# A fused attention and gated-MLP kernel: two of four float32-score pairs become split pairs, the others are filled to 128 rows, ACT copies out all float32 attention, and half of w_in is converted later

## The chip, the core and the metric

The program runs on one core of a Trainium2 chip. The core has a matrix engine (TensorE, here PE, with its weight loads shown as PEld) and four others that work beside it: VectorE (DVE), ScalarE (ACT), GpSimd (POOL) and SyncE (SP), which here only issues transfers. Each engine runs its own instructions in order and waits on semaphores for the others. The metric is the device time of one execution, in microseconds; smaller is better.

## The reference

Eight batches of eight heads, 576 tokens, 64 features a head. Attention is causal with a decay of the key's distance, and its output is the input `x` of a gated MLP (d_model 512, d_ff 1024).

```python
scores = scale * q @ k.T + (cum[i] - cum[j])      # cum = cumsum(log(clip(f, 1e-4, 1)))
attn   = softmax(causal(scores));  x = attn @ v   # (8, 576, 512) after joining heads
h = relu(x @ w_in);  u, v = h[..., :512], h[..., 512:]
v_n = (v - mean(v)) / sqrt(var(v) + 1e-6)
v_s = w_spatial @ v_n (over tokens) + b_spatial
out = (u * v_s) @ w_out
```

All arrays come as float32, but w_in and w_out arrive in HBM as 64-bit words, and the kernel itself turns each 64-bit number into float32 parts.

## The kernel before

**Pairs.** Two heads form a pair; there are 32 pairs `P`, four to a batch. For each pair and head `h` the kernel computes the scores of four query blocks of 128 rows (widths 128, 256, 384, 512; the causal part only) and one joint "tail" for the last 64 rows of both heads (two tiles of 288 columns). DVE takes each score tile out of PSUM with mask and running minimum (line 264, tile `tt`, numbered tt_94 for the first head and tt_95 for the second in the tables below; the tail is `tl`), ACT does the exponential (266), POOL divides by the row sum (274), PE transposes the result (`tp`, 320 and 333), and ACT or DVE copies it to SBUF (`ef`, or `eh` and `el`). `attend` multiplies with v into PSUM (`x`), and ACT and DVE split the result into a rounded part and a rest, `xh` and `xl` (368, 369).

**Three kinds of number.** PE multiplies plain float32, or a rounded form (fp32r) that needs fewer passes. A value is therefore often split into a rounded part and a rest, and a product is then a sum of fp32r products. Early pairs are not split:

- pairs with `P < NQ` (0 to 3) take their scores in float32: one table `ta` (called `tf`) per head with 64 rows of q and k and 2 rows of decay, 66 rows in all, loaded directly by two SP transfers;
- the other pairs are split: `split` loads `raw`, ACT rounds it to `hi` (210), POOL makes `lo` (212), and six SP transfers per head build the tables `ta` (128 rows) and `tb` (68 rows); the scores are the sum of two fp32r products;
- pairs with `P < NF` (0 to 4) use float32 attention: the transposed scores are copied once, to `ef`, and multiplied once. `evac` alternates these copies between ACT and DVE.

**The tables' slots.** `ta` and `tb` have two buffers each, one per head. A head's table for pair P+1 can be loaded only when pair P's scores and tail are done.

**The MLP.** `moe(b)` needs the four pairs of batch b. It computes v (20 groups of products in 512 columns, `ps`), normalizes it on DVE, ACT and POOL, computes u (in 256 and 320 columns), multiplies v by w_spatial (`sph`, `spl`), gates, and multiplies by w_out.

**The weights.** `load64` turns a piece of a 64-bit matrix into a rounded part and a rest: one load on SP, an absolute value on ACT (141), five steps on DVE (142 to 148), a sum on POOL (149), a rounding on ACT (150), and a subtraction on POOL (151). The v half of w_in is converted by `load_first` in four pieces of 512 columns, together with w_spatial. The u half (eight chunks of 256 elements a partition, `load_rest`) and w_out (eight more) follow. A load of such a chunk carries a `mark`: an earlier instruction after which the scheduler is told to place it. It sets the order of the program and is no semaphore.

**What sets the order.** The loops at the end record attention and MLP interleaved by estimated costs; then the framework's scheduler, with a timeline of its own, orders each engine's instructions. So an edit in one place moves instructions elsewhere. During pairs 0 to 3 there is no MLP work to run beside attention.

Of the kernel before, what the change touches and what calls it, by code (L numbers as in the profile page):

```python
# [8 lines left out]
F32 = mybir.dt.float32  # L9
# [8 lines left out]

BIG = 1.0e9
NF = 5  # L20
NQ = 4
LEAD = 0.25
S = 576
D = 64
# [5 lines left out]
QK = 640 + S  # L30
# [3 lines left out]
def f32(ap):  # L34
    return ap.bitcast(F32)
# [3 lines left out]
def attn_gmlp_kernel(ctx: ExitStack, tc: tile.TileContext, qk, v, f, w_in, w_sp, b_sp, w_out, out):  # L39
# [8 lines left out]
    PPB = NPAIR // B  # L48
# [3 lines left out]
    wk = ctx.enter_context(tc.tile_pool(name="wk", bufs=1))  # L52
# [4 lines left out]
    V, A, G, T, SY = nc.vector, nc.scalar, nc.gpsimd, nc.tensor, nc.sync  # L57
# [123 lines left out]
    def load_rest(n, w_v, dh, dl, tag, bufs):  # L181

        raw = mo.tile([128, NJ, 64, 2], U32, name="w64", tag=("gt0", "gt1", "o")[n % 3], bufs=1)
        w = mo.tile([128, NJ, 64], U32, name="w32", tag=tag, bufs=bufs)
        t = mo.tile([128, NJ, 64], U32, name="wa", tag=tag, bufs=bufs)
        c = slice(64 * n, 64 * n + 64)
        load64(w_v[:, :, c, :], dh[:, :, c], dl[:, :, c], raw, w[:], t[:])


    tt = [cst.tile([128, 1280], F32, name=f"tt{h}") for h in range(2)]  # L190
# [2 lines left out]
    ET = {"f": cst.tile([128, 2, 1600], F32, name="ef", tag="eh")}  # L193
# [3 lines left out]
    def mm(o, l, r, st, sp):  # L197
        T.matmul(o, l, r, start=st, stop=sp)  # L198
# [3 lines left out]
    def split(P):  # L202

        if P < NQ:
            return
# [9 lines left out]
    def prep(P, h):  # L215

        p = slice(64 * h, 64 * h + 64)
        if P < NQ:
            ta = wk.tile([66, QK], F32, name="tf", tag="ta", bufs=2)
            SY.dma_start(out=ta[0:64, :], in_=qk[P, p, :])  # L220
            last['dma', P, h] = SY.dma_start(out=ta[64:66, :], in_=r0s[0][32 * h + P:32 * h + P + 1])
            tab[P, h] = (ta,)
            return
        hi, lo = parts[P]
        ta = wk.tile([128, QK], F32R, name="ta", tag="ta", bufs=2)
        tb = wk.tile([128, QK], F32R, name="tb", tag="tb", bufs=2)
        SY.dma_start(out=f32(ta[0:64, :]), in_=hi[p, :])
        SY.dma_start(out=f32(ta[64:128, 0:640]), in_=lo[p, 0:640])
        SY.dma_start(out=f32(ta[64:128, 640:QK]), in_=hi[p, 640:QK])
        SY.dma_start(out=f32(tb[0:64, 0:640]), in_=hi[p, 0:640])  # L230
        SY.dma_start(out=f32(tb[0:64, 640:QK]), in_=lo[p, 640:QK])
        SY.dma_start(out=f32(tb[64:68, :]), in_=rows_v[:, P, h, :])
        tab[P, h] = (ta, tb)
# [12 lines left out]
    def qkt(o, P, h, q0, k0, n, first, final):  # L246

        k0 += 640
        ts = tab[P, h]
        for t in ts:  # L250
            r = 66 if len(ts) == 1 else 128 if t is ts[0] else 68
            mm(o, t[0:r, q0:q0 + 128], t[0:r, k0:k0 + n], first and t is ts[0], final and t is ts[-1])

    def scores(P, h):
# [43 lines left out]
                            op0=ALU.mult, op1=ALU.mult)  # L298
        yield 0

    nev = [0]

    def evac(P, ps, sel):
        if P < NF:
            (V.tensor_copy if nev[0] % 2 == 1 else A.copy)(sel(ET["f"]), ps)  # L305
            nev[0] += 1
            return
        h_ap, l_ap = sel(ET["h"]), sel(ET["l"])
        A.copy(h_ap, ps)  # L309
        V.tensor_tensor(out=l_ap, in0=ps, in1=f32(h_ap), op=ALU.subtract)  # L310
# [65 lines left out]
    def attention(b, ws=None):  # L376
        for P in range(b * PPB, (b + 1) * PPB):
# [15 lines left out]
            if nxt:  # L393
                prep(P + 1, 0)
                prep(P + 1, 1)
# [28 lines left out]
    def moe(b):  # L424
# [55 lines left out]
        if b == 0:  # L480
            for n in range(8):
                load_rest(n, wo_v, woh, wol, 'GH', 3)
# [77 lines left out]
    for n in range(8):  # L560
        load_rest(n, win_v, winh, winl, 'U', 9)
# [52 lines left out]
```

## Time and profile before

| | |
|---|---|
| timed runs | 813.99, 815.69, 815.85 us, median 815.69 |
| profiled execution | 813.26 us, of which the span of the core's instructions is 811.5 |
| mean granted PE clock | 0.985 |
| busy in the span | PE 788.3 (97%), PEld 704.9, DVE 567.1 (70%), ACT 535.2 (66%), POOL 478.1 (59%) |
| DMA | 103.50 MB, mean 128 GB/s |
| pair 0's attention copied out by ACT | second head 48.23 to 48.65 us |
| pair 3's | 97.43 to 97.85 us |
| pair 5's | 156.13 to 156.55 us |

The share of busy time is an average over very different stretches. What the change touches lies in the first 160 us, where the pairs 0 to 5 and the first MLP run, so the stretches between the times of the last three rows tell more than the whole. Busy time of PE counts matmuls with modelled ends, and at half the granted clock a matmul takes twice as long.

### The profile page before, as it was taken

The numbers are of one execution on the slowest core, as the hardware profiler recorded it, in microseconds if no ns is written. First come the engines' busy times: TensorE is split into PE (matmuls) and PEld (weight loads), VectorE is DVE, ScalarE is ACT, GpSimd is POOL, SyncE is SP. The second block draws the span as 40 slices with busy tenths as digits, with TensorE's granted clock in tenths as the row PEclk, the third lists the DMA queues.
The fourth block names the chain that finished last, engine by engine and source line by source line (L and its number), as shares of the span: only waits on it lengthen the run. The fifth ranks groups of instructions, "written<-read, shape, count | busy, mean of one in ns | idle before, by whom it ended". The sixth has DMA issues, their size and how long they took to land.

```text
span 811.5 us, 15566 instructions
## 1 busy us (share of the span) xinstructions
PE 788.3 (97%) x4980; PEld 704.9 (87%) x4980; DVE 567.1 (70%) x1726; ACT 535.2 (66%) x1432; POOL 478.1 (59%) x677
## 2 busy tenths in 40 slices
PE   7999899999999999999999999999999999999997
PEld 3676678998899989998799989999899988999996
DVE  5879989676976668766776668776786658765321
ACT  5587668676776667666686667776687657764431
POOL 4767788655766647555775537566675547643151
PEclk8699999999999999999999999999999999999999
DMA  7547754456545554565554565556554664430001
GB/s 201 143 121 208 197 140 116 120 151 165 139 122 135 135 146 117 128 166 140 125 141 112 150 152 126 123 144 151 131 130 107 163 164 111 95 77 14 27 1 66
DMA packets 47476, 103.50 MB, mean 128 GB/s; under 512 B 6961, under 2 KB 15153, under 8 KB 47330
## 3 DMA queue, kind: packets, MB, share of 16 engines
q1 hardware_dynamic: 47074, 101.98, 49.8%
q8 instruction: 40, 0.66, 0.3%
q10 hardware_dynamic: 320, 0.52, 0.3%
q14 instruction: 42, 0.34, 0.1%
HBM read 39.41 MB, written 10.68 MB: 62 GB/s over the span
## 4 chain that ended last, share of the span: by engine, by line
PE 87%; DVE 5%; POOL 2%; ACT 2%; DMA 2%; issue 1%; SPq 0%; ACTq 0%; POOLq 0%; DVEq 0%
PE ps L198 47%; PE sc L198 16%; PE x L198 12%; PE tp L320 8%; PE tp L198 2%; PE tp L333 2%; DMA out_dram<-o 1%; POOL tt L274 1%; DVE w L145 1%; ACT tt L266 1%; DVE tt L264 1%; DVE eh L342 0%; DVE wa L142 0%; DVE ef L305 0%; DMA w<-in_dram 0%
## 5 line engine op out<-in xcount | busy, mean ns | idle before, releaser
L274 POOL TENSOR_SCALAR tt<-tt,sm 128x128 f32<-128x128 f32 (+3 forms) x256 | 138.3, 558 | 94.7 <-DVE sm L270 86.4
L264 DVE CUSTOM_DVE_ANT_0 tt<-sc,zm 128x128 f32<-128x128 f32 (+3 forms) x256 | 122.4, 485 | 82.4 <-PE tp L320 63.0
L309 ACT CAST eh<-tp 128x512 fp32r<-128x512 f32 (+1 forms) x270 | 111.5, 425 | 87.2 <-PE tp L320 52.5
L266 ACT ACTIVATE tt<-tt,nm 128x128 f32<-128x128 f32 (+3 forms) x256 | 144.4, 565 | 26.5 <-DVE nm L264 21.5
L310 DVE TENSOR_TENSOR el<-tp,eh 128x512 fp32r<-128x512 f32 (+1 forms) x270 | 127.9, 485 | 25.0 <-ACT eh L309 22.8
L320 PE MATMUL tp<-ident,tt 128*128 128x128 f32 x640 | 113.7, 280 | 1.3 <-DVE ef L305 0.6
L198 PE MATMUL sc<-ta 128*128 128x128 f32 (+1 forms) x336 | 107.8, 327 | 3.9 <-DVE nm L264 3.8
L198 PE MATMUL x<-eh,vt 128*128 128x320 f32 (+4 forms) x378 | 104.5, 287 | 2.7 <-POOL vt L243 1.8
L198 PE MATMUL sc<-tb 68*128 68x128 f32 (+1 forms) x336 | 104.6, 316 | 0.0
L212 POOL TENSOR_TENSOR lo<-raw,hi 128x640 fp32r<-128x640 f32 (+1 forms) x56 | 83.2, 1506 | 18.5 <-ACT hi L210 18.4
L505 POOL TENSOR_TENSOR gl<-u,gh 128x256 fp32r<-128x256 f32 x64 | 47.2, 738 | 79.3 <-ACT gh L504 76.1
L198 PE MATMUL x<-el,vt 128*128 128x256 f32 x324 | 93.4, 306 | 0.0
L320 PEld LDWEIGHTS tp<-ident,tt 128*128 128x128 f32 x640 | 76.8, 142 | 10.9 <-ACT ef L305 1.2
L198 PEld LDWEIGHTS x<-eh,vt 128*128 128x128 f32 x378 | 71.2, 189 | 5.8 <-POOL vt L243 2.7
L198 PE MATMUL ps<-sph,vnh 128*128 128x256 f32 (+1 forms) x240 | 73.3, 306 | 0.2 <-ACT o L530 0.2
L198 PE MATMUL ps<-sph,vnl 128*128 128x256 f32 (+1 forms) x240 | 71.4, 298 | 0.0
L198 PEld LDWEIGHTS sc<-ta 128*128 128x128 f32 x336 | 63.5, 189 | 9.1 <-DVE nm L264 4.9
L198 PE MATMUL ps<-spl,vnh 128*128 128x256 f32 (+1 forms) x240 | 71.2, 296 | 0.0
L198 PE MATMUL ps<-xh,winh 128*128 128x256 f32 (+1 forms) x232 | 70.1, 302 | 0.1
L198 PE MATMUL ps<-xl,winh 128*128 128x256 f32 (+1 forms) x232 | 68.9, 297 | 0.0
L368 ACT CAST xh<-x 64x256 fp32r<-64x256 f32 (+1 forms) x128 | 49.8, 392 | 28.4 <-PE x L198 26.9
L198 PE MATMUL ps<-xh,winl 128*128 128x256 f32 (+1 forms) x232 | 68.4, 295 | 0.0
(190 smaller groups left out, 2127.8 us busy)
## 6 DMA issues: line engine op xcount, KB each, us to landing
raw<-in_dram SPq DMA_DIRECT2D x28, 608.0 KB
ta<-hi SPq DMA_DIRECT2D x56, 304.0 KB
vraw<-in_dram SPq DMA_DIRECT2D x32, 320.0 KB
tb<-hi SPq DMA_DIRECT2D x56, 160.0 KB
ta<-lo SPq DMA_DIRECT2D x56, 160.0 KB
out_dram<-o SPq DMA_DIRECT2D x32, 256.0 KB
ta<-hi SPq DMA_DIRECT2D x56, 144.0 KB
tb<-lo SPq DMA_DIRECT2D x56, 144.0 KB
```

The costliest lines, as they stand in the source:

```text
L145: V.scalar_tensor_tensor(out=w, in0=hi, scalar=0xC0000000, in1=a, op0=ALU.bitwise_and, op1=ALU.bitwise_or)
L198: T.matmul(o, l, r, start=st, stop=sp)
L212: G.tensor_tensor(out=lo[:, c], in0=raw[:, c], in1=f32(hi[:, c]), op=ALU.subtract)
L264: V.tensor_tensor_reduce(out=t, in0=sc[:, 0:n], in1=zm[:, 640 - n:640], scale=-0.125, scalar=3.0e38, op0=ALU.add, op1=ALU.min, accum_out=n ...
L266: last["exp", P, h, i] = A.activation(t, t, AF.Exp, bias=nm[:, i:i + 1], scale=-1.0, accum_out=sm[:, i:i + 1])
L274: G.tensor_scalar(out=t, in0=t, scalar1=sm[:, i:i + 1], scalar2=1.0, op0=ALU.mult, op1=ALU.mult)
L309: A.copy(h_ap, ps)
L310: V.tensor_tensor(out=l_ap, in0=ps, in1=f32(h_ap), op=ALU.subtract)
L320: T.transpose(out=tp[:, (i - c) * 128:(i - c + 1) * 128], in_=tt[h][:, TOFF[i] + 128 * c:TOFF[i] + 128 * c + 128], identity=ident)
L333: T.transpose(out=tp[:, j * 128:(j + 1) * 128], in_=tl[:, c * 128:(c + 1) * 128], identity=ident)
L368: last[P, h] = A.copy(hi, ps[m0:m0 + 64, 0:n])
L505: G.tensor_tensor(out=gl[j][:, 0:256], in0=g[:, 0:256], in1=f32(gh[j][:, 0:256]), op=ALU.subtract)
```

## The change

There are four edits.

1. `NQ` goes from 4 to 2: pairs 2 and 3 are now split pairs like the later ones.
2. The float32 tables of pairs 0 and 1 get 128 rows: DVE clears rows 64 to 127 (the memset is recorded ahead of the transfers, and the two decay rows then overwrite rows 64 and 65), and the products run over 128 rows instead of 66.
3. All copies of float32 attention out of PSUM are done by ACT.
4. The loads of `load_rest` get a mark: chunk n of the u half of w_in (and of w_out) comes after the exponential of pair 3, head n // 4, block n % 4.

```diff
-NQ = 4
+NQ = 2
+NPAD = 2
...
-        load64(w_v[:, :, c, :], dh[:, :, c], dl[:, :, c], raw, w[:], t[:])
+        load64(w_v[:, :, c, :], dh[:, :, c], dl[:, :, c], raw, w[:], t[:], ("exp", PPB - 1, n // 4, n % 4))
...
-            ta = wk.tile([66, QK], F32, name="tf", tag="ta", bufs=2)
+            ta = wk.tile([128, QK], F32, name="tf", tag="ta", bufs=2)
+            if P < NPAD:
+                V.memset(ta[64:128, :], 0.0)
...
-            r = 66 if len(ts) == 1 else 128 if t is ts[0] else 68
+            r = (128 if P < NPAD else 66) if len(ts) == 1 else 128 if t is ts[0] else 68
...
     def evac(P, ps, sel):
         if P < NF:
-            (V.tensor_copy if nev[0] % 2 == 1 else A.copy)(sel(ET["f"]), ps)
-            nev[0] += 1
+            A.copy(sel(ET["f"]), ps)
             return
```

The lines of the new program are shifted by one to three (264 becomes 267, 142 becomes 143). What the scheduler makes of it is seen in the order of the instructions. On DVE, at the start of the program, before (`wa` and `w` are tiles of the weights' conversion, `ISA tt_94` is the first score tile's eviction, `r_114` and `rt` are the decay rows):

```order
L100 TENSOR_SCALAR ft<-ft 64x576
L85 MEMSET r_114 32x2x64 x2
L103 SCALAR_TENSOR_TENSOR r_114<-ones,ft 64x576
L89 COPY r_114<-r_114 64x512
L85 MEMSET rt 32x4x64 x2
L142 TENSOR_SCALAR wa<-wa 128x512
L144 TENSOR_SCALAR wa<-wa 128x512
L264 ISA tt_94,nm<-sc,zm 128x128
```

The same place after:

```order
L222 MEMSET tf 64x1216 x2
L101 TENSOR_SCALAR ft<-ft 64x576
L86 MEMSET r_114 32x2x64 x2
L86 MEMSET rt 32x4x64 x2
L104 SCALAR_TENSOR_TENSOR r_114<-ones,ft 64x576
L90 COPY r_114<-r_114 64x512
L267 ISA tt_94,nm<-sc,zm 128x128
```

The clearing of two tables is new, the clearing of `rt` moved ahead of the scan, and the conversion steps moved behind the first score tiles. On PE, at the end of pair 0's second head, where pair 2's scores begin, before (`x` is attention's output in PSUM):

```order
L198 MATMUL x_403<-ef,vraw 128x256
L198 MATMUL sc<-tf 128x128
L198 MATMUL x_403<-ef,vraw 128x128
L320 MATMUL tp<-ident,tt_94 128x128 x7
```

and after:

```order
L199 MATMUL x_414<-ef,vraw 128x256
L199 MATMUL sc<-ta 128x128
L199 MATMUL sc<-tb 128x128
L199 MATMUL x_414<-ef,vraw 128x128
L320 MATMUL tp<-ident,tt_94 128x128
```

One float32 score product became two split ones, with the transposes of pair 1 cut into smaller groups behind. On DVE, the first conversion of a chunk of w_in's u half, before, between the score tiles of pair 2's second head:

```order
L264 ISA tt_95,nm<-sc,zm 128x384
L264 ISA nm 128x1
L305 COPY ef<-tp 128x128
L142 TENSOR_SCALAR wa<-wa 128x256
L144 TENSOR_SCALAR wa<-wa 128x256
L145 SCALAR_TENSOR_TENSOR w_946<-w_945,wa 128x256
L264 ISA tt_95,nm<-sc,zm 128x512
```

and after, between those of pair 4's second head:

```order
L273 RECIPROCAL sm<-sm 128x4
L143 TENSOR_SCALAR wa<-wa 128x256
L145 TENSOR_SCALAR wa<-wa 128x256
L146 SCALAR_TENSOR_TENSOR w_1008<-w_1007,wa 128x256
L294 TENSOR_SCALAR sm<-sm 128x1
L148 TENSOR_SCALAR wa<-w_1008 128x256
L295 RECIPROCAL sm<-sm 128x1
L149 SCALAR_TENSOR_TENSOR wa<-w_1007,wa 128x256
L267 ISA tt_95,nm<-sc,zm 128x384
```

The conversions moved behind by two pairs, and the copy `ef` is gone from DVE.

More of the change, by code (lines that the diff above doesn't have):

```diff
@@ L299, in scores_tail @@
         yield 0
-    nev = [0]
     def evac(P, ps, sel):
         if P < NF:
-            (V.tensor_copy if nev[0] % 2 == 1 else A.copy)(sel(ET["f"]), ps)
-            nev[0] += 1
+            A.copy(sel(ET["f"]), ps)
             return
```

## The prediction

> **What bounds the kernel now.** I read the stretches first. They are cut where ACT has copied out the attention of pair 0 (48.6 us), pair 3 (97.8, from where moe(0) can run) and pair 5 (156.5); I call them A to E. Columns: stretch, its length, busy us of PE, PEld, DVE, ACT, POOL (instructions), granted PE clock, DMA share, GB/s.
>
> ```profile
> 0.00:13.70 13.70, 9.18 (x32) 3.79 (x32) 5.11 (x13) 6.93 (x12) 8.03 (x19) 0.95 0.84 245
> 13.70:48.60 34.90, 34.24 (x110) 23.03 (x111) 27.67 (x83) 21.08 (x58) 22.79 (x26) 0.68 0.46 122
> 48.60:97.80 49.20, 44.51 (x220) 31.73 (x219) 44.84 (x147) 36.02 (x104) 37.22 (x48) 1.00 0.70 188
> 97.80:156.50 58.70, 55.63 (x364) 50.03 (x363) 51.18 (x140) 38.25 (x103) 44.50 (x63) 1.00 0.56 138
> 156.50:811.50 655.00, 644.74 (x4260) 596.37 (x4258) 438.28 (x1346) 432.88 (x1159) 365.57 (x524) 1.00 0.48 120
> ```
>
> E is 98% PE with DVE at 67%: there only PE's work counts, and by PE's order the two programs run alike from pair 11 on. So the change is decided in A to D. In B PE is 98% busy, but at a clock of 0.68. In C PE and DVE stand at 90% and 91% together. D is PE at 95% with DVE at 87%. Second view, the clock inside B (same columns), and third the chain of what ended last:
>
> ```profile
> 11.00:13.70 2.70, 0.15 (x1) 0.00 (x0) 1.08 (x5) 0.88 (x2) 0.00 (x0) 0.76 1.39 418
> 13.70:33.70 20.00, 19.96 (x43) 12.53 (x44) 15.73 (x48) 10.77 (x31) 12.74 (x14) 0.50 0.47 120
> 33.70:36.20 2.50, 2.50 (x11) 2.17 (x9) 2.43 (x3) 0.62 (x1) 1.41 (x1) 0.50 0.77 168
> 36.20:40.00 3.80, 3.18 (x17) 2.06 (x17) 3.23 (x13) 1.96 (x5) 2.58 (x3) 0.99 0.67 211
> PE 87%; DVE 5%; POOL 2%; ACT 2%; DMA 2%; issue 1%; SPq 0%; ACTq 0%; POOLq 0%; DVEq 0%
> ```
>
> For 22.5 us PE is full and gets half its clock. The work there is mostly float32 scores with 66 rows; the clock returns right after 2.5 us of transposes and `x` products with 128 rows. Such work at full clock would take 11.3 us less.
>
> **The start (A).** Rows: start, duration, engine.
>
> ```profile
> 3.51 0.81 DVE L100 TENSOR_SCALAR ft<-ft 64x576 f32<-64x576 f32 x1 [2.07 <-DMA ft<-in_dram]
> 3.96 1.47 POOL L82 MEMSET rt<- 64x1280 f32 x1
> 5.07 1.35 DVE L103 TENSOR_TENSOR_SCAN r<-ones,ft 64x576 f32<-64x576 f32 x1 [0.39 <-ACT ft L101]
> 12.59 0.43 DVE L142 TENSOR_SCALAR wa<-wa 128x512 f32<-128x512 f32 x1 [5.01 <-ACT wa L141]
> 13.39 0.28 DVE L264 CUSTOM_DVE_ANT_0 tt<-sc,zm 128x128 f32<-128x128 f32 x1
> 13.74 2.07 PE L198 MATMUL sc<-tf 66*128 66x512 f32 x2 [2.59 <-DVE nm L264]
> L97 DVE MEMSET ones<- 64x576 f32 x1 | 0.5, 538 | 0.9 <-PEq L600 0.9
> L85 DVE MEMSET rt<- 32x256 f32 x2 | 0.5, 272 | 0.1
> ```
>
> Before, the first score tile is taken out only at 13.39, because two conversion steps stand ahead of it on DVE and wait for a DMA through ACT; PE loses 2.59 us. After, that tile stands ahead of them: the 2.59 us go. Against it, the `rt` memsets of DVE (2 x 0.27) now stand ahead of the scan and wait for POOL's memset of the same rows, which ends at 5.43: the scan starts near 6.0 instead of 5.07, and SP, PE and everything queued wait that 1 us. The four new memsets of 1216 columns cost at most 538 x 1216/576 = 1.14 us each; the first two stand where DVE waits 2.07 us for `ft`, so they hide; the other two add 2.2 us to DVE in B. They also wait for PE to free the tile, with score evictions queued behind, and SP's row transfer waits for them; PE has pair 0's second head to do meanwhile. A: -2.6 + 1.0 = -1.6 us.
>
> **Scores of pairs 2 and 3.**
>
> ```profile
> 50.12 1.14 PE L198 MATMUL sc<-tf 66*128 66x288 f32 x4
> 51.09 0.39 PE L333 MATMUL tp<-ident,tl 128*128 128x128 f32 x2
> 86.89 0.30 PE L198 MATMUL sc<-tb 68*128 68x288 f32 x1
> 87.30 0.60 PE L320 MATMUL tp<-ident,tt 128*128 128x128 f32 x4
> L210 ACT CAST hi<-raw 128x1216 fp32r<-128x1216 f32 x28 | 33.6, 1201 | 0.0
> L212 POOL TENSOR_TENSOR lo<-raw,hi 128x640 fp32r<-128x640 f32 (+1 forms) x56 | 83.2, 1506 | 18.5 <-ACT hi L210 18.4
> ```
>
> Two float32 products of 288 columns run from 50.12 to 51.09, 1.68 ns a column. Three split ones run from 86.89 to 87.30, 0.475 ns a column, and two are needed: 0.95. A pair has 2 x 1280 + 4 x 288 = 3712 columns: 6.25 us become 3.52, so PE saves 5.5 us over two pairs. Each pair adds one cast on ACT (1.2 us) and two subtractions on POOL (3.0 us), and on SP 12 table transfers and one load in place of four. All of this sits in B and C, ahead of moe(0); what hides it is that ACT, POOL and SP have gaps there, and where those close is counted below.
>
> **Evictions.** All 50 float32 copies go to ACT, 25 of them from DVE (14 in C).
>
> ```profile
> L305 DVE COPY ef<-tp 128x128 f32<-128x128 f32 (+2 forms) x14 | 5.7, 407 | 0.4 <-PE tp L320 0.2
> L305 ACT COPY ef<-tp 128x384 f32<-128x384 f32 x5 | 2.3, 465 | 0.0
> L305 ACT COPY ef<-tp 128x256 f32<-128x256 f32 x10 | 3.7, 368 | 0.1
> ```
>
> On ACT 384 columns take 0.465 and 256 take 0.368, so 128 about 0.27 (estimate by the slope): 5 x 0.465 + 6 x 0.27 + 3 x 0.368 = 5.0 us in C. DVE loses 5.7 there, 0.41 x 6 = 2.4 in B and 0.41 x 5 = 2.1 in D.
>
> **Later conversion of w_in.** One chunk of 256 columns costs DVE 2.70 us (five rows), ACT 0.82, POOL 1.54:
>
> ```profile
> L142 DVE TENSOR_SCALAR wa<-wa 128x256 f32<-128x256 f32 x16 | 9.6, 603 | 2.9 <-ACT wa L141 2.9
> L145 DVE SCALAR_TENSOR_TENSOR w<-w,wa 128x256 uint32<-128x256 uint32 x16 | 9.5, 591 | 0.3
> L144 DVE TENSOR_SCALAR wa<-wa 128x256 uint32<-128x256 uint32 x16 | 8.8, 548 | 0.1
> L148 DVE SCALAR_TENSOR_TENSOR wa<-w,wa 128x256 f32<-128x256 uint32 x16 | 8.6, 536 | 0.1
> L147 DVE TENSOR_SCALAR wa<-w 128x256 uint32<-128x256 uint32 x16 | 6.8, 425 | 0.1
> L141 ACT ACTIVATE wa<-w 128x256 f32<-128x256 f32 x16 | 6.9, 431 | 2.8 <-DMA w<-in_dram 2.8
> L150 ACT CAST winh<-w 128x256 fp32r<-128x256 f32 x8 | 3.1, 392 | 0.0
> L149 POOL TENSOR_TENSOR w<-w,wa 128x256 f32<-128x256 f32 x16 | 12.7, 792 | 13.3 <-DVE sm L269 6.7 <-DVE wa L148 5.0 <-DVE sm L270 1.6
> L151 POOL TENSOR_TENSOR winl<-w,winh 128x256 fp32r<-128x256 f32 x8 | 5.9, 744 | 0.0
> 97.39 2.73 PE ps L198 x11
> 100.12 0.76 PE tp L320 x7
> ```
>
> By DVE's order 5 chunks instead of 8.5 stand ahead of pair 3's last product, and about 2.5 more in D; the rest of w_out's chunks slides into E, where DVE has room. On SP the eight loads of w_in stood between the tables of pairs 3 to 5, now between those of pairs 4 to 6; each waits there for its slot with the next tables queued behind, as before, so I put nothing for SP. PE's order also pulls 11 moe products and 7 transposes (the last two rows, 3.5 us) ahead of pair 3's end, and drops 25 spatial products behind pair 5 (net some 1.3 us, my count of PE's rows).
>
> **The sum, stretch by stretch** (after, in us of work):
> - B: DVE 27.7 - 2.4 + 2.2 + 0.9 (two conversion steps that no longer run in A) = 28.4; PE 34.2 - 11.3 = 22.9 if the padded rows keep the clock up; ACT and POOL under 26. DVE takes over. At the 91% it reached in C: 31 instead of 34.9, -4.0. Bounds: 28.4 (-6.5, no gaps) and 34.9 (0, clock as before).
> - C: PE 44.5 - 5.5 + 3.5 = 42.5; ACT 36.0 + 5.0 + 2.4 (two more casts) - 3.7 (4 x 0.431 and 5 x 0.392) = 39.7; POOL 37.2 + 6.0 - 6.9 = 36.3; DVE 44.8 - 5.7 - 9.5 = 29.6. PE at 92%, with ACT close behind it: 46.2, -3.0. Bounds: 43 (-6) and 50 (+1, ACT at 80%).
> - D: PE 55.6 - 3.5 - 1.3 = 50.8; DVE 51.2 - 2.1 + 6.8 = 55.9, the new bound, at 95%: 59.0, +0.3. Bounds: 54 (PE at 95%) and 66 (DVE at 85%).
> - E: +1.3, since PE is the bound.
>
> Sum: -1.6 - 4.0 - 3.0 + 0.3 + 1.3 = -7.0. The profiled execution took 813.26 us, so 806.3 beside it. The three timed runs have their median 2.4 above it (815.69) and the fastest 0.7 above; I put half of that on top: **807.5 us**.
>
> **Rivals.**
> 1. The clock does not follow the rows. For it: the added rows are zeros and PE was already 100% busy; against it: 22.5 us at 0.50 that ended with 128-row work, which weighs more. Then B stays 34.9 and the time is about 811.5. It costs only 4 us, since DVE is close behind. The Trainium skill, "TensorE: Matmul & The Clock Gate", Part 1, says that about 3.4 us of sustained PE activity lifts the clock from half to full, without naming rows. By that rule the fill would do nothing; the 20 us row at 0.50 with PE full does not agree with it.
> 2. The engines fill their gaps better than I allow, with the lower bounds throughout: -1.6 - 6.5 - 6 - 4.7 + 1.3 = -17.5, about 797. For it: DVE in C ran at 91% with conversions as filler. Against it: in C four engines now stand within 13 us, and ACT's copies are all on the path.
> 3. Slower: conversions clog D. They share DVE with layer norm, softmax and the gate, and winl and wol come out of POOL last; PE's u-phase and w_out tiles need all of a chunk's columns. If DVE reaches only B's 79% in D (27.67/34.90), D takes 71, +12, and the sum is +5: about 820. It decides once D exceeds 66. Against it: DVE ran 87% in D before, with 8 such chunks.
> 4. No change: tables of split pairs come late. Before there is no wait of PE on `ta` or `tb`, but with moe's work as cover from pair 4 on; in C there is none. One head's six transfers take SP from 87.14 to 91.58:
>
> ```profile
> 87.14 0.47 SPq L227 DMA_DIRECT2D ta<-hi  x1
> 90.90 0.68 SPq L231 DMA_DIRECT2D tb<-lo  x1
> ```
>
> With 4.4 us of issue and a head's slot freed only by the tail scores, 1.5 to 2 us for each of four heads would cost 6 to 8: about 814.
>
> **How the numbers follow.** Forecast 0.45 (803 to 811), rival 1 0.15, rival 2 0.15, rival 3 0.13, rival 4 0.12. About 0.3% (2.4 us) is what a measurement of this kernel can tell from no change. Forecast and rivals 1 and 2 are faster (0.75), rival 4 is the same (0.12), rival 3 slower (0.13). The range 798 to 816 leaves out rival 3 and the better part of rival 2's lower half, 0.13 and 0.06.
>
> **What would show it.** Clock near 1.00 from 14 us on, with DVE, not PE, full in 12 to 43; no 2.59 us wait of PE at the first scores; pair 0 done near 43, pair 3 near 89, pair 5 near 148; no waits of PE on `ta` or `tb`; ACT the busiest after PE in C, DVE in D. Wrong if PE waits for winl or wol (rival 3), or for transfers (rival 4), or if the clock is 0.50 after 20 us (rival 1).

## The result: 1.6% slower, and the profile after

The changed kernel takes 827.65 us (median; 825.44 to 829.84) beside 815.04 us of the kernel before, a ratio of 1.0159 with a 95% interval of 1.0142 to 1.0175. The forecast was 807.5 us. The profiled execution of the changed kernel took 829.84 us with a span of 828.0; it is the slowest of its four, and the profiled one of before (span 811.5) was a quick one, so the stretches below add up to 16.5 us where the medians differ by 12.6. In the tables below S is the split of pairs 2 and 3 (`NQ = 2`), F the fill to 128 rows, A the evictions by ACT alone.

First the stretches, cut at the same events as before (the columns are those of the prediction: length, busy us of PE, PEld, DVE, ACT, POOL, granted clock, DMA share, GB/s):

```profile
0.00:13.70 13.70, 10.74 (x38) 4.95 (x38) 7.35 (x14) 6.68 (x11) 9.09 (x19) 1.00 0.65 199
13.70:47.10 33.40, 25.83 (x118) 17.35 (x116) 28.51 (x83) 24.90 (x71) 25.86 (x28) 0.95 0.78 203
47.10:105.40 58.30, 47.03 (x244) 37.54 (x245) 40.85 (x116) 39.56 (x113) 35.46 (x45) 0.91 0.73 186
105.40:167.00 61.60, 52.50 (x312) 46.47 (x311) 55.22 (x146) 41.27 (x112) 50.06 (x65) 0.92 0.53 136
167.00:828.00 661.00, 648.57 (x4274) 599.61 (x4272) 443.18 (x1348) 431.95 (x1156) 367.10 (x527) 1.00 0.48 119
```

| | before | after | difference | forecast |
|---|---|---|---|---|
| A and B, to the end of pair 0 | 48.6 | 47.1 | -1.5 | -5.6 |
| C, to the end of pair 3 | 49.2 | 58.3 | +9.1 | -3.0 |
| D, to the end of pair 5 | 58.7 | 61.6 | +2.9 | +0.3 |
| E, the rest | 655.0 | 661.0 | +6.0 | +1.3 |

The first row needs a closer look. In the timelines (start, duration), pair 0's last products on PE, first of the kernel before, then of the changed one, and behind them ACT's copy of the latter:

```profile
47.12 0.85 PE L198 MATMUL x<-ef,vraw 128*128 128x192 f32 x4
40.81 2.47 PE L199 MATMUL x<-ef,vraw 128*128 128x320 f32 x10
46.70 0.42 ACT L368 CAST xh<-x 64x320 fp32r<-64x320 f32 x1
```

PE has done pair 0 at 43.28 instead of 47.97, 4.7 us earlier. ACT copies it only at 46.70: it works without a pause from 42.60 on, and three casts of weights are among what stands ahead of the copy. So the head start was there, and was gone by the time the next pairs could use it.

Over two thirds of the loss lies in C and D. There PE is busy 81% and 85% of the time instead of 90% and 95%, and its clock, which was 1.00 throughout before, is 0.91 and 0.92. The two belong together, as a finer cut shows (same columns):

```profile
45.00:48.00 3.00, 0.14 (x2) 0.02 (x1) 0.17 (x2) 2.38 (x7) 3.00 (x6) 1.00 0.98 241
48.00:50.00 2.00, 1.86 (x12) 1.68 (x13) 1.30 (x5) 2.00 (x3) 2.00 (x2) 0.98 0.11 37
50.00:52.00 2.00, 1.89 (x9) 1.39 (x7) 2.00 (x1) 0.80 (x4) 2.00 (x3) 0.50 0.83 167
52.00:55.00 3.00, 0.00 (x0) 0.00 (x0) 2.94 (x3) 0.72 (x2) 2.23 (x2) 0.50 0.46 96
55.00:60.00 5.00, 4.84 (x11) 3.37 (x12) 0.79 (x7) 1.73 (x7) 2.05 (x4) 0.50 0.57 120
60.00:62.00 2.00, 2.00 (x13) 1.54 (x11) 1.09 (x6) 1.60 (x6) 1.36 (x2) 0.96 0.82 236
140.70:144.50 3.80, 0.10 (x2) 0.05 (x1) 3.67 (x5) 0.70 (x3) 3.04 (x3) 1.00 0.92 187
144.50:149.00 4.50, 4.50 (x23) 4.50 (x24) 4.02 (x17) 2.34 (x6) 3.69 (x9) 0.62 0.90 266
```

PE stands still for 3 us (45 to 48), and two us later the clock is halved, although it is busy again; it stands still once more (52 to 55), and stays at 0.50 to 60 us. The same follows the gap at 141 to 144 us. What made these gaps? In C, the waits of PE (who waited for whom: us, times, longest):

```profile
PE sc L199 <- DVE nm L267: 3.4, 2, 3.3
PE sc L199 <- DMA ta<-hi: 2.9, 1, 2.9
PE sc L199 <- DMA ta<-lo: 2.0, 1, 2.0
PE x L199 <- DMA vraw<-in_dram: 2.0, 1, 2.0
PE sc L199 <- DMA tb<-lo: 1.7, 1, 1.7
```

8.6 us are waits for transfers (2.0 of them ahead of 47.10), of which before had none but 0.2 us at the start. The two longest waits stand in the engines' own rows (start, duration):

```profile
36.70 0.35 SPq L208 DMA_DIRECT2D raw<-in_dram  x1
37.09 1.39 SPq L164 DMA_DIRECT2D wraw<-in_dram  x3
38.58 0.61 SPq L230 DMA_DIRECT2D ta<-hi  x1
48.01 0.37 PE L199 MATMUL sc<-ta 128*128 128x288 f32 x1 [2.87 <-DMA ta<-hi]
47.37 2.78 POOL L166 TENSOR_TENSOR spl<-wraw,sph 128x576 fp32r<-128x576 f32 x2
49.55 4.70 DVE L292 TENSOR_TENSOR nm<-nm 128x1 f32<-128x1 f32 x1
50.11 1.27 POOL L152 TENSOR_TENSOR winl<-w,winh 128x512 fp32r<-128x512 f32 x1
51.35 2.88 POOL L213 TENSOR_TENSOR lo<-raw,hi 128x640 fp32r<-128x640 f32 x2
55.16 0.80 PE L199 MATMUL sc<-ta 128*128 128x512 f32 x1 [3.27 <-DVE nm L267]
```

The table of pair 2's second head is issued from 38.58 us on, behind a raw table and three pieces of w_spatial, and PE waits for it to 48.01. Then DVE takes 4.70 us for a minimum of two single columns, which takes 0.15 us elsewhere in the same run. It ends at 54.25, just when POOL ends the last of a row of subtractions that it had begun at 47.37 and run without a pause. The next score tile is evicted only behind it, and PE waits 3.27 us.

In D, conversions of the weights stand ahead of the MLP's work on DVE, stretched beside POOL in the same manner:

```profile
138.95 1.32 DVE L145 TENSOR_SCALAR wa<-wa 128x256 uint32<-128x256 uint32 x1
140.37 1.58 DVE L146 SCALAR_TENSOR_TENSOR w<-w,wa 128x256 uint32<-128x256 uint32 x1
141.98 1.24 DVE L148 TENSOR_SCALAR wa<-w 128x256 uint32<-128x256 uint32 x1
143.72 0.68 DVE L450 TENSOR_TENSOR vx<-ps,vx 64x512 f32<-64x512 f32 x1
137.13 3.00 POOL L213 TENSOR_TENSOR lo<-raw,hi 128x640 fp32r<-128x640 f32 x2
140.09 1.58 POOL L246 TENSOR_TENSOR vt<-vraw,vt 128x640 fp32r<-128x640 f32 x1
141.63 1.44 POOL L460 TENSOR_TENSOR vnl<-vx,vnh 128x512 fp32r<-128x512 f32 x1
144.45 0.39 PE L199 MATMUL ps<-xh,winh 128*128 128x256 f32 x1 [3.69 <-DVE vx L450]
```

These steps had means of 0.55, 0.59 and 0.43 us in the run before; here they take 1.32, 1.58 and 1.24, each ending within 0.3 us after a subtraction of POOL (140.27 and 140.13, 141.95 and 141.67, 143.22 and 143.07), and PE waits 3.69 us for an addition behind them.

### The profile page after: what moved, and what is told of

The parts are those of the page before. It is cut to its first block, busy times and chain, and to the rows that moved or that the text cites. A ratio compares the mean times of both kernels' runs of the same rounds, so it can differ in the third digit from the quotient of the medians.

```text
span 828.0 us, 15624 instructions
## 1 busy us (share of the span) xinstructions
PE 784.7 (95%) x4980; PEld 705.9 (85%) x4980; DVE 575.1 (69%) x1705; ACT 544.4 (66%) x1459; POOL 487.6 (59%) x681
## 4 chain that ended last, share of the span: by engine, by line
PE 75%; DVE 3%; ACT 1%; POOL 1%; issue 1%; DMA 1%; ACTq 0%; DVEq 0%; POOLq 0%
PE ps L199 43%; PE sc L199 12%; PE x L199 9%; PE tp L320 7%; PE tp L199 2%; PE tp L333 2%; DMA out_dram<-o 1%; DVE el L310 0%; POOL vt L246 0%; POOL lo L213 0%; DVE vx L456 0%; DVE eh L342 0%; ACT eh L309 0%; DVE tt L267 0%; ACT hi L211 0%
## 5 line engine op out<-in xcount | busy, mean ns | idle before, releaser
L199 PE MATMUL sc<-ta 128*128 128x128 f32 (+1 forms) x360 | 117.6, 334 | 14.8 <-DVE nm L267 9.5
L199 PE MATMUL sc<-tb 68*128 68x128 f32 (+1 forms) x360 | 113.0, 320 | 1.7 <-DMA tb<-lo 1.7
L213 POOL TENSOR_TENSOR lo<-raw,hi 128x640 fp32r<-128x640 f32 (+1 forms) x60 | 89.1, 1505 | 23.7 <-ACT hi L211 23.4
L199 PEld LDWEIGHTS sc<-ta 128*128 128x128 f32 x360 | 68.6, 191 | 23.2 <-DVE nm L267 13.5
L199 PEld LDWEIGHTS sc<-tb 68*128 68x128 f32 x360 | 69.0, 192 | 4.2 <-DMA tb<-lo 2.0
```

The costliest lines, as they stand in the source:

```text
L213: G.tensor_tensor(out=lo[:, c], in0=raw[:, c], in1=f32(hi[:, c]), op=ALU.subtract)
```

## The experiments

**How they are compared.** Each time stands over the median of the kernel before on the same chip. For the profiled execution of each I also add up two losses of PE to 240 us, where the first batches are done: idle time, and time lost to half clock (busy time x (1 - clock)), both over stretches of 1 us. For before and after the rows of the whole stretch give the same within the rounding of the clock:

```profile
0.00:240.00 240.00, 225.74 (x1257) 184.03 (x1258) 190.49 (x573) 163.75 (x438) 165.29 (x227) 0.95 0.59 152
0.00:240.00 240.00, 205.87 (x1136) 169.34 (x1137) 184.45 (x516) 159.37 (x430) 162.26 (x215) 0.94 0.62 160
```

Before: 240 - 225.7 = 14.3 idle, 225.7 x 0.05 = 11.3 lost. After: 34.1 idle, 205.9 x 0.06 = 12.

| kernel | edits | us over before | ratio, 95% interval | idle | half clock | span less both |
|---|---|---|---|---|---|---|
| before | | 0 | | 14.3 | 11.2 | 786.0 |
| after | S F A, mark | +12.6 | 1.0142 to 1.0175 | 34.1 | 11.3 | 782.6 |
| e1 | F A, mark | +1.6 | 0.9997 to 1.0023 | 18.5 | 3.3 | 793.5 |
| e2 | S F, mark | +6.0 | 1.0053 to 1.0110 | 27.6 | 13.5 | 780.9 |
| e3 | S A, mark | +9.1 | 1.0088 to 1.0137 | 21.5 | 17.6 | 781.5 |
| e4 | S | +9.6 | 1.0093 to 1.0142 | 19.3 | 22.9 | 780.3 |
| e5 | F | +5.3 | 1.0046 to 1.0079 | 24.4 | 6.2 | 787.8 |
| e6 | A | +1.3 | 1.0003 to 1.0026 | 15.7 | 13.5 | 786.1 |
| e7 | after, w_spatial later | +15.9 | 1.0146 to 1.0218 | 35.3 | 9.9 | 783.3 |
| e8 | after, one-input minimum | +7.0 | 1.0073 to 1.0103 | 29.9 | 6.6 | 782.2 |
| e9 | after, lo on DVE | +6.1 | 1.0055 to 1.0094 | 25.2 | 11.8 | 781.8 |
| e10 | S, one-input minimum | +3.7 | 1.0031 to 1.0064 | 20.8 | 17.7 | 779.2 |
| e11 | before, lo on DVE | +2.0 | 1.0010 to 1.0033 | 13.9 | 13.3 | 788.2 |
| e12 | S F, mark, one-input minimum | +11.2 | 1.0119 to 1.0156 | 30.1 | 7.5 | 786.4 |
| e13 | e10, constant tables | +0.7 | 0.9993 to 1.0039 | 23.4 | 11.4 | 778.8 |
| e14 | pair 3 split, one-input minimum | +3.8 | 1.0028 to 1.0064 | 20.4 | 12.9 | 784.6 |
| e15 | F, lo on DVE | +4.3 | 1.0034 to 1.0064 | 21.5 | 3.2 | 793.4 |
| e16 | S, one-input minimum, lo on DVE | +11.5 | 1.0108 to 1.0162 | 20.2 | 21.0 | 781.6 |
| e17 | e10, 32 filler matmuls | +6.0 | 1.0046 to 1.0079 | 17.4 | 13.1 | 788.8 |
| e18 | F for four pairs, A, mark | +2.5 | 1.0018 to 1.0043 | 21.5 | 4.7 | 788.5 |

Two things hold over the whole table. The kernels that split both pairs (without e17) have 778.8 to 786.4 in the last column, median 781.6; those that split none have 786.0 to 793.5, median 788.2. The last column also holds the idle time behind 240 us, some 9 us in each; PE's busy time times its clock, added up over the whole span, gives 771.1 for the split alone (e4) and 777.1 before. So the saving of matmul time is there, about 6 us of it. And the sum of idle time and half clock is 34.8 to 45.4 us with both pairs split, 21.8 to 30.6 with none. The split buys some 6 us for some 13.

In the kernel before, only the loads of `load_first` carry a mark; the fourth edit gives one to those of `load_rest`. In the changed program, in e2 and in e3 it does nothing: without it, every engine has the same instructions in the same order. In e1 and e18, which do not split pairs 2 and 3, it does change the order, and no run has these two without it. So before, after and e1 to e6 are the eight combinations of S, F and A with one reservation: e1 is F and A and a mark that counts. And one thing comes with the split in every run: the first chunk of w_in's u half reaches DVE at 68 to 92 us in the kernels that split both pairs, and at 59 to 64 in those that split none. No run splits without this delay, so its share of the split's price is not told apart.

### Parts taken back: e1, e2, e3

```diff
e1  -NQ = 2                        +NQ = 4
e2  -            A.copy(sel(ET["f"]), ps)
    +            (V.tensor_copy if nev[0] % 2 == 1 else A.copy)(sel(ET["f"]), ps)
    +            nev[0] += 1
e3  -NPAD = 2                      +NPAD = 0
```

> The changed kernel with NQ back at 4: pairs 2 and 3 again use one float32 table each, read with 66 rows; the 128 rows of pairs 0 and 1, ACT's evictions and the mark stay. Theory T (the split tables of pairs 2 and 3 are late: TensorE waited 8.6 us for transfers and 3.4 us for VectorE between 47.1 and 105.4 us): those waits go, the stretch from the end of pair 0 to that of pair 3 falls from 58.3 us to about 50, and the time from 827.6 to 811-817. Rival A (ACT as the only one to take out the float32 attention is what costs): 824-830, the stretch stays above 56. Rival F (the fill costs): 824-830.

> The changed kernel with the float32 evictions again shared between ACT and VectorE in turn; pairs 2 and 3 stay split, pairs 0 and 1 keep 128 rows. Theory T (late split tables): within 3 us of the changed kernel, 824-830, and the waits of TensorE for ta and tb stay. Rival A (ACT alone is too slow for the evictions): most of the loss goes, 815-820.

> The changed kernel without the fill: pairs 0 and 1 use 66 rows and no memsets; the rest stays. Theory T: the granted clock between 13.7 and 47.1 us falls from 0.95 to about 0.7 and pair 0 ends 1 to 3 us later, while the later stages stay as they are: 827-832. Rival F (memsets and full rows cost more than the clock gives): faster than the changed kernel by over 2 us, 820-825.

Without the split the changed kernel takes 816.05 us: 11.0 of the 12.6 us are gone. Idle time to 240 us falls from 34.1 to 18.5, and stretch C, between the same events, from 58.3 to 48.3 us. Its row, and below it that of e8, an experiment further down:

```profile
45.95:94.26 48.31, 42.84 (x218) 31.22 (x216) 40.03 (x129) 38.83 (x114) 35.91 (x46) 1.00 0.71 186
49.03:99.57 50.54, 46.02 (x241) 37.27 (x240) 32.95 (x110) 38.35 (x108) 34.27 (x44) 0.93 0.87 217
```

Idle time and half clock of C together are 5.5 us in e1, where after has 11.3 + 4.2 = 15.5. That is theory T, with e1's mark as the reservation. But the other two did not stay within its lines: sharing the evictions gives 6.6 us back (820.47), and leaving out the fill 3.5 (823.59), where T wanted no change and a loss. With 66 rows the clock did fall (12.7 us lost up to 50 us, in place of 1.5), yet idle time to 240 us fell by 12.6 at the same time.

### Parts alone: e4, e5, e6

```diff
e4  -NQ = 4                        +NQ = 2
e5  the fill's lines of the change, with NQ = 4
e6  the eviction's lines of the change
```

> The kernel before with NQ = 2 as its only edit: pairs 2 and 3 split, pairs 0 and 1 with 66 rows, evictions in turn, no mark. Theory T: this edit alone brings the loss, 823-832, with waits of TensorE for ta or tb between pair 1 and pair 3. Rival (the loss needs ACT's evictions or the fill beside it): 808-818; by the terms of the prediction, the split alone takes about 3 us off, 812.

> The kernel before with the fill as its only edit: the tables of pairs 0 and 1 hold 128 rows, and scores of them read 128; NQ stays 4. Before lost 11.2 us of matmul time to a granted clock of 0.5, all of it between 13 and 37 us; the kernel with the whole change but for the split lost 3.3. Theory C (the clock follows the rows, and what is won there is kept in part): 811-814. Rival (the faster scores only wait longer for VectorE, and the memsets cost 2 us at the head): 814-818.

> The kernel before with the evictions as its only edit: ACT alone takes out the float32 attention. Theory E (ACT, 73% busy before pair 3's end, becomes late for the transposed scores and for the exponentials behind them): 817-821. Rival (it only moves work between two engines that both wait): 813-816.

The split alone loses 9.6 us (824.13), as T says, and PE waits 3.5 us for split tables between 40 and 110 us; the prediction's own term for it, 812, is out. It loses by clock more than by idle time: 22.9 us at half clock beside 11.2. The fill alone loses 5.3 us (819.16), against theory C and above its rival's 818 too: the half clock falls from 11.2 to 6.2, and idle time rises from 14.3 to 24.4. ACT's evictions alone cost 1.3 us (815.20), and E is out.

Over the eight combinations, the split costs 9.6, 0.7 (with F), 7.8 (with A) and 11.0 (with both), 7.3 in the mean; the fill +5.3, -3.6 (with S), +0.3 (with A), +3.5 (with both), mean 1.4; ACT's evictions +1.3, -0.5 (with S), -3.7 (with F), +6.6 (with both), mean 0.9. The split's 11.0, the fill's +0.3 and the evictions' -3.7 rest on e1. Only the split has one sign, and its 0.7 with F is within the intervals of e2 and e5. For the others the price depends on what stands beside them; each combination is also another order of the program, and I take the spread of some 10 us for that, without a run that shows it alone.

### What the fill wins and where it goes

The losses cut at 50 us, from the same sums (idle plus half clock):

| with and without the fill | to 50 us | 50 to 240 us |
|---|---|---|
| e5 and before | 11.5, 16.4 | 19.1, 9.1 |
| e2 and e4 (split) | 14.7, 16.8 | 26.4, 25.4 |
| after and e3 (split, ACT) | 13.1, 19.6 | 32.3, 19.5 |
| e1 and e6 (ACT) | 9.7, 16.7 | 12.1, 12.5 |

In each pair the fill wins 2.1 to 7.0 us up to 50 us, around the 5.6 of the forecast. In two of the four it is kept (beside S by half), in two more than lost behind. In e5 one place of the loss is again an operation of DVE that stands still while POOL makes `lo`:

```profile
134.74 3.53 DVE L149 SCALAR_TENSOR_TENSOR wa<-w,wa 128x256 f32<-128x256 uint32 x1
135.09 2.90 POOL L213 TENSOR_TENSOR lo<-raw,hi 128x640 fp32r<-128x640 f32 x2
138.80 0.61 PE L199 MATMUL sc<-ta 128*128 128x288 f32 x1 [2.52 <-DVE nm L267]
```

After that wait the clock was at 0.5 for 7 us. Before, no operation of DVE up to 170 us was stretched by more than 1.5 us.

### The transfers: e7

```diff
-            after(SY.dma_start(out=raw, in_=w_sp[c * 128:(c + 1) * 128, :]), (0, 0))
+            after(SY.dma_start(out=raw, in_=w_sp[c * 128:(c + 1) * 128, :]), ("exp",) + ((2, 0, 3), (2, 1, 3), (3, 0, 3), (3, 1, 0))[c])
```

> The changed kernel with the four loads of w_spatial held until exponentials of pairs 2 and 3, so that they are issued behind the tables of pair 2; nothing else is edited. In the changed kernel three of them (0.86 MB) and a raw table of 0.62 MB were issued at 36.7 to 38.5 us, ahead of the table for which TensorE then waited from 45.1 to 48.0 us. Theory D (the split tables queue behind the weights): the wait for ta and tb at 45 us goes and no clock of 0.5 follows at 50 us, 820-825. Rival (tables are late because of the work that makes them): waits and time stay, 826-830.

829.83 us, no gain. The 2.87 us wait at 45 us went, and no half clock followed until 79 us. But idle time to 50 us stayed as it was (11.7 and 11.6), and later came two waits for `ta`, 3.6 us together, and one of 6.1 us for ACT. Theory D is not borne out: moving these loads out of the way moved the gaps.

### DVE beside POOL: e8, e9, e10, e11, e12, e16

```diff
e8, e10, e12, e16
-        V.tensor_tensor(out=nm[:, 2:3], in0=nm[:, 0:1], in1=nm[:, 1:2], op=ALU.min)
+        V.tensor_scalar(out=nm[:, 2:3], in0=nm[:, 0:1], scalar1=nm[:, 1:2], scalar2=None, op0=ALU.min)
e9, e11, e16
-            G.tensor_tensor(out=lo[:, c], in0=raw[:, c], in1=f32(hi[:, c]), op=ALU.subtract)
+            (V if P < 8 else G).tensor_tensor(out=lo[:, c], in0=raw[:, c], in1=f32(hi[:, c]), op=ALU.subtract)
```

> The changed kernel with the minimum of two columns (line 292, 128x1) written as an operation with one tensor and a per-partition scalar, in place of two tensors. In the changed kernel it took 4.70 us, to the end of four operations that GpSimd ran without a pause, and TensorE then waited 3.3 us. Theory P (VectorE's second input is kept out while GpSimd runs): it takes under 0.5 us, TensorE's wait there falls below 1 us, 822-826. Rival (any form of it waits, or the wait moves to the next operation): 826-830.

> The changed kernel with the subtraction that makes lo (line 213) on VectorE instead of GpSimd for the pairs below 8; nothing else is edited. Theory P (operations of VectorE with tensors in SBUF stand still while GpSimd runs without a pause, and the 2.9 us of lo are the longest of such runs): no operation of VectorE is stretched by over 2 us before 170 us, the 4.70 us of line 292 fall below 1.5 us, TensorE's idle time falls from 43 us to below 40, and the time is 818-824. Rival (VectorE, the busiest after TensorE there, pays for six more subtractions): 827-833.

> The kernel before with NQ = 2 and the minimum of line 289 as an operation with one tensor. With NQ = 2 alone that minimum took 4.18 us at 52.8 us and the kernel 824.1. Theory P: half or more of the loss of the split goes with it, 815-820. Rival (the split loses by its longer way from load to table, and the minimum only happened to stand there): 822-826.

> The kernel before with the subtraction that makes lo on VectorE for the pairs below 8. In it no operation of VectorE before 170 us was stretched by over 1.5 us. Theory P: little to win, 812-815. Rival (VectorE is what bounds the stage to the end of pair 3, 44.8 us busy of 49.2): four subtractions of about 1.4 us lie on the path there, 817-821.

> The changed kernel with both the one-input minimum and the evictions shared again; split and fill stay. Each alone took 6.8 and 7.2 us off the changed kernel. If they mend different things: 813-816. If both mend the same stall of VectorE by moving what meets what: 818-822.

> The kernel before with NQ = 2, the one-input minimum and lo on VectorE for the pairs below 8. Theory P (the stall is most of what is left): 811-815, and no operation of VectorE stretched by over 2 us before 170 us. Rival (the stall is dealt with by the minimum alone, the rest is another cause): 816-820.

The stall of the minimum is as theory P has it. With the split alone (e4) the same minimum stood still again, to the end of POOL's row of subtractions (52.84 + 4.18 = 57.02; 55.61 + 1.40 = 57.01), and as an operation with one tensor (e8, last row) it takes 0.21 us in the same place of the program:

```profile
52.84 4.18 DVE L289 TENSOR_TENSOR nm<-nm 128x1 f32<-128x1 f32 x1
52.73 2.92 POOL L212 TENSOR_TENSOR lo<-raw,hi 128x640 fp32r<-128x640 f32 x2
55.61 1.40 POOL L165 TENSOR_TENSOR spl<-wraw,sph 128x576 fp32r<-128x576 f32 x1
51.10 0.21 DVE L292 TENSOR_SCALAR nm<-nm 128x1 f32<-128x1 f32 x1
```

But a hold can move on. In e10, the split alone with the minimum mended (0.21 us there too), the next operation of 128x4 is held in the same place, again to the end of POOL's row (53.59 + 2.84 = 56.43; 54.98 + 1.42 = 56.40), so that 2.84 us stand where 4.18 stood; in e8 no operation up to 170 us is stretched by more than 1.4 us:

```profile
53.59 2.84 DVE L269 TENSOR_SCALAR sm<-sm 128x4 f32<-128x4 f32 x1 [0.16 <-ACT tt L266]
52.10 2.94 POOL L212 TENSOR_TENSOR lo<-raw,hi 128x640 fp32r<-128x640 f32 x2
54.98 1.42 POOL L165 TENSOR_TENSOR spl<-wraw,sph 128x576 fp32r<-128x576 f32 x1
```

The Trainium skill, "SBUF — State Buffer", "Who interferes with whom", says that an instruction of DVE with two inputs in SBUF is kept out by one of GpSimd that reads SBUF, and one with a single input, outside of certain faster modes, is not. The 4.70 and 0.21 us agree; that the wait lasts over several of POOL's instructions, where these follow without a pause, is more than the page tells.

The price of the stall is less clear. One edit of one line takes 5.6 us off the changed kernel (820.86, e8, more than theory P's range has), where C falls to 50.5 us with 7.7 of idle time and half clock, and 5.9 off the split alone (818.29, e10), though a hold is still there; taking `lo` off POOL takes 6.5 off the changed kernel (820.67, e9). The sum does not follow: with the evictions shared, the one-input minimum makes the kernel 5.2 us slower than e2 (825.73, e12); both edits together on the split alone give 826.22 (e16), 7.8 us more than e10, with no operation of DVE stretched by more than 1.2 us; and on the kernel before, `lo` on DVE costs 2.0 us (816.53, e11). So edits against the stalls are worth some 6 us in the changed kernel, each with a new order of the program beside it, and no fixed price follows: e16, without a stall, has 21.0 us of half clock, 9.6 of them after 50 us, behind other waits of PE, none above 2.5 us.

### The way to the tables, one pair, fill with lo: e13, e14, e15

```diff
e13 (on e10, in split)
+        if P == 1:
+            hi = wk.tile([128, QK], F32R, name="hi", tag="hi")
+            G.memset(f32(hi[:]), 0.5)
+            parts[2] = parts[3] = (f32(hi[:]), f32(hi[:]))
-        if P < NQ:
+        if P < 4:
             return
e14 (one-input minimum)            -NQ = 4        +NQ = 3
e15 the fill's lines with NQ = 4, and lo as in e9
```

> The kernel of e10 (split of pairs 2 and 3, one-input minimum), with the split tables of pairs 2 and 3 copied from one constant tile made at the start: their raw loads, casts and subtractions are left out, the table transfers, and all of TensorE's work, stay; scores of pairs 2 and 3 are those of constants. Theory W (the way from load to table is the rest of the split's loss): idle and half-clock time up to 240 us falls from 38.5 us to 28 or less, and the time from 818.3 to 806-811. Rival (the transfers themselves, or VectorE behind the scores, set the pace): 815-819.

> The kernel before with NQ = 3 and the one-input minimum: only pair 3 is split. The split of one pair saves 3 us of matmul time. Theory W (pair 2's tables are due while the way to them is crowded by the first weights; pair 3's have a pair's time more): most of the loss goes, 811-815. Rival (each split pair loses the same): 816-818.

> The kernel before with the fill of pairs 0 and 1, and lo on VectorE for the pairs below 8. With the fill alone (819.2) two operations of VectorE were stretched to 3.5 us beside lo, and TensorE, 4.9 us ahead at 50 us, had lost 10 us behind it by 240 us. If the gain was lost to these stalls: 809-813. If it is lost because TensorE only reaches work sooner that waits for the weights' conversion: 815-819.

Without the loads, casts and subtractions of pairs 2 and 3 the kernel takes 815.47 us: 3.0 less than e10, not the 7 to 12 of theory W; the sum of the losses falls from 38.5 to 34.8, not to 28. That is most of the 3.7 us by which e10 is behind before, and e13 is level with before within its interval (0.9993 to 1.0039); but of the 13.0 us that e10 loses more than before in idle time and half clock (38.5 beside 25.5) only 3.7 go. The way to the tables is a part of the split's cost, and not the greater one. One split pair (818.48) loses as much as two (818.29) with the same minimum: theory W is out here too, and the time is just above its rival's. The fill with `lo` on DVE (818.97) is no better than the fill alone, although its losses to 240 us are 24.7 us, below before's 25.5: its other time is 793.4, as in e1. In both, the tail from pair 11's last copy of `xh` takes 516 and 517 us in place of 512, so an advance of the head is no gain if the rest is ordered worse.

### Is PE's time the bound at all? e17 and e18

```diff
e17 (on e10, in scores)
+            for _ in range(2 if P in (2, 3) else 0):
+                mm(sc, zm[:, 0:128], zm[:, 0:512], True, True)
             qkt(sc[:, 0:n], P, h, q0, 0, n, True, True)
e18 (on the changed kernel)        -NQ = 2 -NPAD = 2      +NQ = 4 +NPAD = 4
```

> The kernel of e10 (split of pairs 2 and 3, one-input minimum) with 32 matmuls of constants added, two ahead of each of the 16 score tiles of rows of pairs 2 and 3; the following matmul overwrites them. At the 0.29 us that the 26 at the start of the kernel before took (7.6 us) they are 9.4 us of TensorE's time, more than the 6 us that the split saves. Theory S (the other engines bound that stage, and what the split saves comes back as idle time and, through it, as time at half clock): no slower than e10 by over 2 us, 814-820. Rival (TensorE's time counts there): 824-829.

> The changed kernel with NQ = 4 and NPAD = 4: no pair below 4 split, all four with 128 rows, evictions by ACT. The kernel with the rows of two pairs (e1) was 1.2 us ahead of the kernel before at the end of pair 11 and lost 5 us behind it, in another order of the work; here the order of TensorE's work from pair 11 on is that of the kernel before. If the gain is kept: 810-814. Rival (what is won at the head comes back as waiting in pairs 4 to 7): 815-819.

In e17 PE does 9.7 us of added work in the stage of pairs 2 and 3:

```profile
L198 PE MATMUL sc<-zm 128*128 128x512 bf16 x32 | 9.7, 381 | 0.0
```

The time rises from 818.29 to 819.94 (by 2.3 us when each stands over the kernel before of its own chip), and the profiled span from 817.7 to 819.3. The sum explains it: 9.7 more work, 3.4 less idle time (20.8 to 17.4), 4.6 less half clock (17.7 to 13.1), which makes +1.7. By the time, theory S holds: of 9.7 us more work under 2.5 reach the end. But where the work came back is not the stage itself. The rows from 50 to 100 and from 100 to 180 us, first of e10, then of e17:

```profile
50.00:100.00 50.00, 43.22 (x231) 34.12 (x231) 43.78 (x140) 35.05 (x98) 37.49 (x50) 0.97 0.89 217
100.00:180.00 80.00, 72.51 (x446) 65.28 (x445) 64.68 (x186) 52.52 (x140) 57.05 (x77) 0.94 0.52 135
50.00:100.00 50.00, 44.14 (x245) 33.85 (x244) 43.99 (x143) 36.10 (x100) 37.07 (x48) 1.00 0.86 214
100.00:180.00 80.00, 73.81 (x458) 64.30 (x457) 68.39 (x184) 50.77 (x137) 57.59 (x77) 0.98 0.53 134
```

Some 8 us of the added work lie in the first stretch, and there idle time and half clock, by the sums over 1 us, fall by only 2.7 us (8.5 to 5.8); stretch C is 3.1 us longer than in e10 (49.7 for 46.6). Most of the rest is made up from 100 to 180 us, where the sum falls by 4.2 (12.1 to 7.9). So within the stage PE's time counts in good part; it is the head as a whole that PE's work does not bound, because what comes earlier out of C waits longer behind it. e17 is also another order of the program than e10, as all these runs are. e18, meant to keep the fill's gain, takes 816.46 us, 2.5 over before: it has 11.0 us of both losses up to 50 us, where before has 16.4, and 15.2 from there to 240 us, where before has 9.1. That is its rival's case. None of these kernels beats the kernel before.

## Why the prediction was wrong, point by point

- **Chance and side.** Faster was given 0.75, slower 0.13; it is slower, 11.6 us above the range. The slower side was rival 3's, a clogged D; the largest miss lies in C.
- **A, -1.6.** Both terms came out: the 2.59 us wait for the first score tile is gone, and the first scores wait 1.17 us for the decay rows where it was 0.18, the 1.0 us of the scan.
- **A and B together, -5.6.** PE won 4.7 of it (43.28 for 47.97). That the rows keep the clock up is right, and rival 1 is out: 0.95 in place of 0.68 here, and 12.7 us lost to 50 us as soon as the rows are 66 again (e3); the last section has this over all twenty kernels. That DVE takes over is right to a tenth: 28.51 us of work, 28.4 forecast, and it is busy nearly all of the time to 38 us. What failed here is the tacit step that the next stage starts as much earlier: ACT copied pair 0 out 3.4 us late, and from 45.1 to 48.0 PE waited for a table of pair 2.
- **C, -3.0, the largest miss.** PE's 42.5 us of work were not wrong (47.03 x 0.91 = 42.8). The step that failed is "PE at 92%": it gave a stage with less PE work the share of a stage that PE and DVE had filled together, which leaves 3.7 us for all gaps and none for the clock. Measured are 11.3 us of gaps and 4.2 of half clock. 10.0 us of the gaps are the waits for the split tables and `vraw` and for DVE's evictions, most of it behind the stall, each of which the sum put at nothing; without the split C loses 5.5 us (e1), with the one-input minimum 7.7 (e8), and each of these two is also another order of the program. Even the upper bound, 50 at ACT's 80%, fell short of 58.3.
- **The clock behind a gap, the second term put at nothing.** The forecast let the clock stay at 1.00 in C and D because it was so before, and read the fall in B as a matter of rows only. In the changed kernel 9.8 of its 11.3 us at half clock come after 50 us. The profile before had it in one place: the row of 11.00 to 13.70 us has 0.15 us of work, and the clock is at 0.50 behind it. I read only the rows of the matmuls there, since the later gaps, up to 1.8 us within 3.5, had cost nothing. The Trainium skill, "TensorE: Matmul & The Clock Gate", "HAM oscillation — how this bites in real kernels", tells of idle gaps of TensorE that bring the half clock back, and I weighed only Part 1 of that page. The trace agrees, at shorter gaps (2.87 us here) than the 3.4 us it gives.
- **D, +0.3.** DVE's 55.22 us were forecast as 55.9. It reached 90%, not 95%, by the mechanism of rival 3 in small: conversions ahead of the MLP's steps on DVE, 3.69 us of PE at one place. Its threshold of 66 us was not reached (61.6). The rest of the miss is the clock: 52.50 x 0.08 = 4.2 us.
- **E, +1.3.** It is +6.0, of which 4.4 lie before the end of pair 7 (45.9 us to 202.4 before, 50.3 to 217.3 after). From pair 11 on the two need the same time within 0.4 us.
- **Rival 4** was there, with the waits for `ta` and `tb` that it named, 6.6 us at the scores of C (and 2.0 for `vraw`), as it had priced; only it was put against a gain elsewhere that did not come.
- **The evictions** were treated as free of path, with no cost of their own: right in the mean (0.9 us), not in the single case (-3.7 to +6.6). **The later conversion** is none of the mark's doing; it comes with the split.

What is shown: the split carries most of the loss (e1, e4 and the mean over the eight), though beside F alone it costs 0.7 us; its matmul saving is real, and an advance of PE in the head was lost behind it in e5 and e18, as a lag was made up in e17; each fall of the clock stands behind idle time of PE; the stall of DVE beside POOL is real, and edits against it took 5.6 to 6.5 us off the changed kernel. What stays open: which wait makes up the rest, and what part of it is the later conversion, which no run takes back by itself. Taking a single one away (loads ahead of the tables, the way to them, the stall) mostly moved the gaps elsewhere, and twice (e12, e16) edits against the stall made a kernel 5 to 8 us slower. I put that down to the new order of the program, which differs in every run; none shows it by itself.

## What to carry to other kernels

A stage in which several engines stand near 90% has no single bound, and what one of them saves there has to be followed into the next stage: a run with work added to that engine (e17) shows how much of its time reaches the end, 2 us of 9.7 here. Price a gap of TensorE with the half clock that can follow it, not with its length alone. And where a scheduler orders the program, an edit is to be judged over several combinations with others, since its single price moved by 9 to 10 us here with what stood beside it.

## What the runs showed of the hardware

- **The clock falls in steps of some 3.4 us.** From 24 to 240 us, in after and the 18 experiments, it fell 55 times, and each time for 3.5 to 4, 7 to 7.5 or 10.5 us, read in stretches of half a us (by the clock in each of these, 3.3 to 3.4, 6.7 to 6.8 or 10.2 us). The idle time in the 3.5 us ahead was mostly 1.2 to 3.5 us; gaps of up to 2.6 us within 3.5 passed elsewhere without a fall. The Trainium skill, "TensorE: Matmul & The Clock Gate", Part 1, gives a free-running window of 3413 ns for the decision, which fits the steps and the spread. It does not fit the 22.5 us of full work on 66 rows at 0.50 before.
- **66 rows did not bring the clock back, 128 did.** Near the start, at the scores of the first pairs, the clock falls behind a gap in most kernels, and then it stays at 0.50 for 13.7 to 23.9 us in all ten with 66 rows (before, e3, e4, e6, e10, e11, e13, e14, e16, e17), and for 3.4 or 6.8 us, or does not fall there, in all ten with 128 rows (after, e1, e2, e5, e7, e8, e9, e12, e15, e18).
- **A small operation of DVE can be held for over 4 us.** 128x1 with two tensors: 0.15 us alone, 4.70 and 4.18 beside an unbroken row of POOL's subtractions, ended by their end; with one tensor and a per-partition scalar 0.18 to 0.22 in all its 32 places (e8, e10). Single-tensor operations with a constant were held too: 128x4 for 3.23 us in e5 and 2.84 in e10.
